# Attention and two MLPs on one core: the second MLP's weights are converted to float32 in DRAM beside blocks 1 to 4

## The chip, the core and the metric

The kernel runs on one core of a Trainium2 chip. A core has four engines that compute: TensorE (PE in the profile: matmuls, and PEld, its loading of weights), VectorE (DVE), ScalarE (ACT) and GpSimd (POOL); SyncE (SP) issues the transfers, which 16 DMA engines carry. Each engine works through its own queue in order. The metric is the time of one execution in microseconds (us).

## What is computed

Causal attention with a decay over 4 x 8 heads of 576 positions and 64 columns, then two MLPs on the 2304 x 512 result:

```python
scores = np.where(causal, -1e9, scale * q @ k.T + decay)
x  = softmax(scores) @ v                     # 2304 x 512, after moving heads
h  = x @ w_in                                # first MLP, 512 -> 2048
x  = (h * tanh(softplus(h))) @ w_out         # 2048 -> 512
h  = x @ w2_in                               # second MLP, 512 -> 1024
s  = h * softmax(h)
out = layernorm(s) * g_ln @ w2_out           # 1024 -> 512
```

The weights of both MLPs come as float64; all else is float32.

## The kernel before

Every float32 operand of a matmul is split into two float16 parts (high and low), and three products of parts make one product, so weights have to be converted and split before they are used. The result of attention is cut into 9 blocks of 256 rows (`TB`, `NBLK`). One loop runs over `hn`, two half steps for each of the 144 pieces of the first MLP (16 pieces of its 2048 columns a block): the first half step issues `up` (12 matmuls, line 754), the second one `mish_a` to `mish_c` on ScalarE, VectorE and POOL and `down` (6 matmuls of an earlier piece, line 798). Between them the loop issues the next slots of attention (scores, maximum, exponential, split, transpose by DMA, product with v), which run ahead of the block that needs them; attention ends in block 6.

A chunk of weights is 2 x 128 rows of 512 columns. The first MLP has 16 chunks, the second 8: four of `w2_in`, which go to the tile `w`, and four of `w2_out`, which go to `wo`. `Weight` handles them: `load` (line 123) brings the chunk as float64, 1 MB, into one of two staging buffers (`WB`); `conv` makes float32 of it with three VectorE operations on int32 views (lines 136, 138 and 140), in the place where the split will stand; for `w2_out` two VectorE operations (line 146) multiply the rows by `g_ln`; a square on ScalarE (line 149) leaves the sums from which `bound` takes the scale; `split` (lines 197 to 205) makes the two float16 parts, either with ScalarE and VectorE (`on_pool` 0) or with ScalarE for the scale and POOL for both parts (`on_pool` 1).

The first MLP's 16 chunks go through staging memory (`wst`) in the first 150 us, and that memory is then closed (line 913) and stays unused. When the last slot of attention has been issued, its memory is closed and `Stage2` takes it (here called the handover): its constructor makes a list of 26 steps, of which `prepare` takes one at every third half step (`S2E`): two loads, then conversions and loads in turn for both matrices, and for each matrix the bound and the four splits, all with POOL. When fewer than 9 steps are left (`S2R`) and at least 10 pieces have passed (`S2A`), `step` is called at every third piece: `first` (lines 991 to 1027) does the first product of a tile of 128 rows and all up to the layer norm, `second` (line 1037) the last product. What is left of the 18 tiles after the loop is done by `rest`.

The rows of the code are written in this order, and the program's scheduler then places each engine's instructions in the order in which it expects them to become ready; the queues run in that order.

## Time and profile before

| | |
|---|---|
| time, median of 3 runs (lowest, highest) | 861.41 us (856.87, 861.95) |
| the profiled execution's own time | 862.0 us |
| its span, first to last instruction | 860.2 us |
| busy: TensorE, VectorE | 748.2 us (87%), 606.7 us (71%) |
| busy: ScalarE, POOL | 549.1 us (64%), 442.2 us (51%) |
| granted TensorE clock, mean | 0.97 |

The shares are means over stages with different limits. In the first 180 us attention's first batch and the first MLP's weights fill VectorE; up to about 540 us the blocks of the first MLP and attention run beside each other; from there to about 600 us the first MLP runs beside the handover; after that the two MLPs, and at the end the second one alone, run on a full TensorE. A change is read from the stage in which it lies.

### The profile page before, as it was taken

How to read it: one execution, taken by the hardware profiler on the slowest of the kernel's cores; microseconds unless marked ns; L12 is line 12 of the kernel's file. 1: busy time of each engine (PE TensorE's matmuls, PEld its weight loads, DVE VectorE, ACT ScalarE, POOL GpSimd, SP SyncE). 2: the span in 40 equal slices, each digit the busy share in tenths (PEclk: the TensorE clock that was granted, in tenths of full speed). 3: DMA queues.
4: the chain of work that ended last, by engine and by line, in shares of the span. 5: the costliest groups of instructions: out<-in, count | busy, mean ns of one | idle time of the engine just before them, and what ended most of it. 6: DMA issues, size and time to landing. Idle time of an engine off the chain costs nothing.

```text
span 860.2 us, 16457 instructions
## 1 busy us (share of the span) xinstructions
PE 748.2 (87%) x6174; PEld 477.6 (56%) x6174; DVE 606.7 (71%) x1158; ACT 549.1 (64%) x1202; POOL 442.2 (51%) x341
## 2 busy tenths in 40 slices
PE   0555777789899988999999999986999999999997
PEld 0444545557567665676757677554555554444443
DVE  6699998597667878858887755599566444665451
ACT  5555657868778786888886767686955554333331
POOL 2268676755876576776678753228733122022110
PEclk9999997789999999999999999999999999999999
DMA  9999554487897889898896632841023423344543
GB/s 237 208 246 271 166 174 92 87 157 120 149 190 157 154 152 161 178 191 140 164 184 124 138 67 56 221 172 62 26 38 79 81 59 75 89 98 104 108 88 81
DMA packets 328571, 114.88 MB, mean 134 GB/s; under 512 B 317676, under 2 KB 317676, under 8 KB 328492
## 3 DMA queue, kind: packets, MB, share of 16 engines
q1 hardware_dynamic: 328492, 113.84, 63.2%
q8 instruction: 48, 0.79, 0.4%
q14 instruction: 31, 0.25, 0.1%
HBM read 46.59 MB, written 9.55 MB: 65 GB/s over the span
## 4 chain that ended last, share of the span: by engine, by line
PE 40%; DVE 23%; DMA 13%; ACT 9%; issue 8%; POOL 7%; SPq 1%; POOLq 0%; DVEq 0%; ACTq 0%
PE h L997 10%; PE o L1037 10%; PE x L798 9%; PE h L754 7%; DMA pT<-ph 4%; POOL ph L493 4%; DVE th L775 3%; DVE ta L771 2%; DMA w2i_r<-in_moe_w_in_dram 1%; DVE wout L140 1%; PE pv L524 1%; DVE ph L490 1%; DVE wout L138 1%; POOL gt L781 1%; DMA rawk<-in_k_dram 1%
## 5 line engine op out<-in xcount | busy, mean ns | idle before, releaser
L798 PE MATMUL x<-wout,gt 128*128 128x512 f16 x864 | 222.1, 392 | 21.8 <-ACT gt L780 10.1
L754 PE MATMUL h<-xT,win 128*128 128x256 f16 x1728 | 223.3, 279 | 2.3 <-POOL win L202 1.7
L493 POOL TENSOR_TENSOR ph<-p,ph 128x512 f16<-128x512 f32 (+4 forms) x120 | 159.6, 1334 | 80.3 <-ACT ph L492 32.8
L754 PEld LDWEIGHTS <-win 128*128 128x128 f16 x1728 | 170.3, 100 | 45.3 <-POOL win L202 1.8
L781 POOL TENSOR_TENSOR gt<-th,gt 128x512 f16<-128x512 f32 x72 | 91.9, 1277 | 100.5 <-ACT gt L780 100.5
L798 PEld LDWEIGHTS <-gt 128*128 128x128 f16 x864 | 81.6, 100 | 103.7 <-issue 14.9
L1025 POOL TENSOR_TENSOR z<-sl,z 128x1024 f16<-128x1024 f32 x18 | 38.7, 2150 | 138.1 <-DVE s2c L1004 111.3
L997 PE MATMUL h<-w,x2T 128*128 128x512 f16 x432 | 98.4, 380 | 2.9 <-POOL w L205 1.6
L1037 PE MATMUL o<-wo,zT 128*128 128x512 f16 x432 | 96.5, 379 | 0.5 <-DMA zT<-z 0.5
L410 PE MATMUL sp<-kt,qa 128*128 128x128 f16 (+3 forms) x480 | 71.8, 225 | 21.1 <-ACT p L454 11.9
L454 ACT ACTIVATE p<-sp,nm 64x64 f32<-64x64 f32 (+7 forms) x128 | 61.2, 484 | 41.0 <-DVE nm L452 23.3
L524 PE MATMUL pv<-vt,pT 128*128 128x64 f16 (+3 forms) x480 | 71.0, 203 | 15.4 <-DMA pT<-ph 10.7
L775 DVE SCALAR_TENSOR_TENSOR th<-ta,th 128x512 f32<-128x512 f32 x72 | 69.4, 965 | 21.1 <-ACT ta L774 20.9
L780 ACT CAST gt<-th 128x512 f16<-128x512 f32 x72 | 44.3, 615 | 48.6 <-DVE th L775 47.2
L411 PE MATMUL sp<-kt,qb 67*128 67x128 f16 (+3 forms) x480 | 72.9, 226 | 2.6 <-DVE qb L399 2.6
L997 PEld LDWEIGHTS <-x2T 128*128 128x128 f16 x432 | 42.3, 98 | 53.9 <-issue 4.0
L525 PE MATMUL pv<-vt,pT 128*128 128x64 f16 (+3 forms) x480 | 70.1, 198 | 1.0 <-DVE vt L198 1.0
L1037 PEld LDWEIGHTS <-zT 128*128 128x128 f16 x432 | 42.2, 98 | 51.5 <-DMA zT<-z 1.0
L526 PE MATMUL pv<-vt,pT 128*128 128x64 f16 (+3 forms) x480 | 70.3, 198 | 0.0
L772 ACT ACTIVATE ta<-ta 128x512 f32<-128x512 f32 x72 | 45.3, 631 | 36.0 <-DVE ta L771 35.8
L524 PEld LDWEIGHTS <-pT 128*128 128x128 f16 (+3 forms) x480 | 45.6, 102 | 36.7 <-DMA pT<-ph 20.5
L771 DVE TENSOR_SCALAR ta<-ta 128x512 f32<-128x512 f32 x72 | 53.7, 745 | 16.6 <-ACT ta L766 16.2
(235 smaller groups left out, 1455.8 us busy)
## 6 DMA issues: line engine op xcount, KB each, us to landing
wi_r<-in_moe_w_in_dram SPq DMA_DIRECT2D x8, 1024.0 KB
wo_r<-in_moe_w_out_dram SPq DMA_DIRECT2D x8, 1024.0 KB
rawk<-in_k_dram SPq DMA_DIRECT2D x25, 256.0 KB
rawv<-in_v_dram SPq DMA_DIRECT2D x25, 256.0 KB
x2d<-x2h SPq DMA_DIRECT2D x18, 256.0 KB
out_dram<-ro SPq DMA_DIRECT2D x18, 256.0 KB
w2i_r<-in_moe_w_in_dram SPq DMA_DIRECT2D x4, 1024.0 KB
w2o_r<-in_moe_w_out_dram SPq DMA_DIRECT2D x4, 1024.0 KB
```

Of the source, the lines that this page charges most:

```text
L410: nc.tensor.matmul(o, qa[:, h, r0:r1_], kc[:, h, a0:a1], start=True, stop=False)
L411: nc.tensor.matmul(o, qb_[:67, h, r0:r1_], kc[:67, H + h, a0:a1], start=False, stop=(c != i))
L493: nc.gpsimd.tensor_tensor(p4[:, :, 1], pv3, p4[:, :, 0], op=ALU.subtract)
L524: nc.tensor.matmul(o, pT[a0:a1, k, :m], vh, start=(c == 0), stop=False)
L526: nc.tensor.matmul(o, pT[a0:a1, k + 1, :m], vh, start=False, stop=(c == i))
L754: nc.tensor.matmul(ph, win[:, (fi // 4) * NC1 + c, col:col + P], x[:, lx * NC1 + c, :], start=(m == 0), stop=(m == 3 * NC1 - 1))
L771: nc.vector.tensor_scalar(ta, ta, E20, 1.0, op0=ALU.min, op1=ALU.add)
L775: nc.vector.scalar_tensor_tensor(th, ta, 2.5, th, op0=ALU.subtract, op1=ALU.mult)
L781: nc.gpsimd.tensor_tensor(gt[:, 1], th, gt[:, 0], op=ALU.subtract)
L798: nc.tensor.matmul(o, gt[:, lg, n % 2, t * P:(t + 1) * P], wout[:, fi, lw * 512:(lw + 1) * 512], start=(first and m == 0), stop=(last and ...
L997: nc.tensor.matmul(h[:, half * 512:(half + 1) * 512], x[:, lx * NC1 + c, :], self.w2[:, half * NC1 + c, lw * 512:(lw + 1) * 512], start=(n ...
L1037: nc.tensor.matmul(o, zT[:, lz * NF2 + c, :], self.wo[:, c, lw * 512:(lw + 1) * 512], start=(n == 0), stop=(n == 3 * NF2 - 1))
```

## The change

A new list of 25 steps, `pre`, is worked off in the loop once the first MLP's staging is closed: one step at every fourth half step from half step 36 on (`S2P0`, `S2PE`). Its first step opens a staging memory of one float64 buffer and one float32 buffer in the room of `wst`. Then each of the 8 chunks has three: its load; its conversion with the same three VectorE operations (now in `to_f32`) and, for `w2_out`, the two row scales; its square, with the float32 chunk's store to a DRAM tile `w2f`. `g_ln` is loaded at the start of the program. What is left of the list when attention ends would be done then.

`Stage2` reads the eight float32 chunks, 0.5 MB each, from `w2f` straight to the places where the splits take them, all eight issued at once, and has 10 steps left: two bounds and eight splits. Every second split uses ScalarE and VectorE and no longer POOL. `prepare` takes a step at every second half step, and the second MLP's tiles may start after 7 pieces and when fewer than 6 steps are left.

```diff
-S2A = 10
+S2A = 7
-S2R = 9
+S2R = 6
-S2E = 3
+S2E = 2
+S2P0 = 36
+S2PE = 4
...
+    def fetch(self, n):
+        self.nc.sync.dma_start(self.f32[:, 2 * n + 2:2 * n + 4].rearrange("p s e -> p (s e)"), self.src(n))
...
+    def pre_open(_):
+        pool = ea.enter_context(tc.tile_pool(name="w2c", bufs=1, side="right"))
+        nc.sync.dma_start(gl, g_ln.rearrange("(f p) -> p f", p=P))
+        wq["raw"] = pool.tile([P, 2, 512], w2_in.dtype, name="w2raw")
+        wq["f"] = pool.tile([P, 2, 512], F32, name="w2f32")
+    def pre_load(a):
+        nc.sync.dma_start(wq["raw"], part_of((w2_in, w2_out)[a[0]], a[1]))
+    def pre_conv(a):
+        w, n = a
+        raw, f = wq["raw"], wq["f"]
+        if raw.dtype != F32:
+            to_f32(nc, f, raw)
...
+        if w:
+            for s in range(2):
+                nc.vector.tensor_scalar(f[:, s], f[:, s], gl[:, 2 * n + s:2 * n + s + 1], None, op0=ALU.mult)
+    def pre_stat(a):
+        w, n = a
+        nc.scalar.activation(
+            wq["raw"].bitcast(F16)[:, :, :512], wq["f"], AF.Square, accum_out=w2st[:, w, n:n + 1])
+        nc.sync.dma_start(w2f[w, n], wq["f"].rearrange("p s e -> p (s e)"))
...
+        if wstp is None and pre and hn >= S2P0 and hn % S2PE == 0:
+            f, a = pre.pop(0)
+            f(a)
         if st2 is None and half and pos["k"] >= len(seq) + LAG:
+            while pre:
+                f, a = pre.pop(0)
+                f(a)
             ea.close()
-            st2 = Stage2(tc, es, w2_in, w2_out, g_ln, x2d, us2, out, ones)
+            st2 = Stage2(tc, es, w2f, w2st, x2d, us2, out, ones)
...
-        self.steps = [(a.load, n) for n in range(WB)]
-        for w, after in ((a, b), (b, None)):
+        for w in (a, b):
             for n in range(w.n):
-                self.steps.append((w.conv, n))
-                if n + WB < w.n:
-                    self.steps.append((w.load, n + WB))
-                elif after is not None:
-                    self.steps.append((after.load, n + WB - w.n))
+                w.fetch(n)
+        self.steps = []
+        for w in (a, b):
             self.steps.append((bound, w))
-            for n in range(w.n):
-                self.steps.append((w.split, n))
+            self.steps += [(lambda n, w=w: w.split(n, on_pool=n % 2), n) for n in range(w.n)]
```

Where the steps stand on the engines is decided by the scheduler. Three places, each as before and as now (line numbers differ, since the changed kernel's lines lie lower: 136, 138 and 140 are now 107, 109 and 111; 338, 96, 98 are 346, 98, 100; 300, 374, 396, 498 are 308, 382, 404, 506).

On VectorE, where the scales of attention's batch 1 are made (`sctkv`), before:

```order
L775 SCALAR_TENSOR_TENSOR th_1864<-ta_1863,th_1864 128x512
L338 TENSOR_SCALAR sctkv_1522<-sp_147 128x2
L96 TENSOR_SCALAR sctkv_1522<-sctkv_1522 128x2
L98 TENSOR_SCALAR sctkv_1522<-sctkv_1522 128x2
L340 RECIPROCAL sctkv_1522<-sctkv_1522 128x2
```

and now:

```order
L783 SCALAR_TENSOR_TENSOR th_1867<-ta_1866,th_1867 128x512
L107 TENSOR_SCALAR w2f_2070<-w2raw 128x1024
L346 TENSOR_SCALAR sctkv_1525<-sp_147 128x2
L109 SCALAR_TENSOR_TENSOR w2f_2070<-w2raw,w2f_2070 128x1024
L98 TENSOR_SCALAR sctkv_1525<-sctkv_1525 128x2
L111 SCALAR_TENSOR_TENSOR w2f_2070<-w2raw,w2f_2070 128x1024
L100 TENSOR_SCALAR sctkv_1525<-sctkv_1525 128x2
```

The second chunk's three operations (on `w2f`, from the staging `w2raw`) stand between the operations that make these scales.

On SP, behind the loads of batch 1's first rows (`rawv_0`), beside the transposes of attention's last rows of batch 0 (`pT`), before:

```order
L300 DMA rawv_0_1730<-in_v_dram 64x8x64
L498 DMA_TRANSPOSE pT_3_2_1193<-ph_3_2_1158 128x16x128
L498 DMA_TRANSPOSE pT_3_4_1288<-ph_3_4_1238 128x16x128
L498 DMA_TRANSPOSE pT_3_6_1382<-ph_3_6_1341 128x16x128
L498 DMA_TRANSPOSE pT_4_0_1504<-ph_4_0_1466 128x20x64
```

and now:

```order
L308 DMA rawv_0_1733<-in_v_dram 64x8x64
L891 DMA w2raw<-in_moe_w_in_dram 128x2x512
L506 DMA_TRANSPOSE pT_3_2_1196<-ph_3_2_1161 128x16x128
L506 DMA_TRANSPOSE pT_3_4_1291<-ph_3_4_1241 128x16x128
L908 DMA w2f<-w2f_2070 128x1024
L891 DMA w2raw<-in_moe_w_in_dram 128x2x512
L506 DMA_TRANSPOSE pT_3_6_1385<-ph_3_6_1344 128x16x128
L506 DMA_TRANSPOSE pT_4_0_1507<-ph_4_0_1469 128x20x64
L908 DMA w2f<-w2f_2070 128x1024
L891 DMA w2raw<-in_moe_w_in_dram 128x2x512
```

Three loads and two stores stand between the transposes; a store waits for its chunk's conversion, and the load behind it for that chunk's square.

On VectorE at the handover, behind the last operations of attention, before (`w2i_r` is a staging buffer, `w` the matrix):

```order
L136 TENSOR_SCALAR w_7366<-w2i_r_7412 128x1024
L138 SCALAR_TENSOR_TENSOR w_7366<-w2i_r_7412,w_7366 128x1024
L140 SCALAR_TENSOR_TENSOR w_7366<-w2i_r_7412,w_7366 128x1024
L771 TENSOR_SCALAR ta_7642<-ta_7642 128x512
L136 TENSOR_SCALAR w_7366<-w2i_r_7475 128x1024
L138 SCALAR_TENSOR_TENSOR w_7366<-w2i_r_7475,w_7366 128x1024
L140 SCALAR_TENSOR_TENSOR w_7366<-w2i_r_7475,w_7366 128x1024
L775 SCALAR_TENSOR_TENSOR th_7643<-ta_7642,th_7643 128x512
```

and now (`w2i_b` holds the first matrix's scale, `s2c` belongs to the second MLP's first tile):

```order
L184 TENSOR_SCALAR w2i_b<-sum_7471 128x1
L98 TENSOR_SCALAR w2i_b<-w2i_b 128x1
L100 TENSOR_SCALAR w2i_b<-w2i_b 128x1
L186 RECIPROCAL w2i_b<-w2i_b 128x1
L1011 TENSOR_SCALAR c_iw_7434<-w2i_b 128x1
L783 SCALAR_TENSOR_TENSOR th_7677<-ta_7676,th_7677 128x512
L187 TENSOR_SCALAR w2i_b<-w2i_b 128x1
L1049 TENSOR_TENSOR s2c_7802<-us_74,c_iw_7434 128x1
L1049 TENSOR_TENSOR s2c_7928<-us_74,c_iw_7434 128x1
L206 SCALAR_TENSOR_TENSOR w_7432<-w_7432,w2i_b 128x2x512
```

The conversions are gone; the first split (line 206) follows the scale of the first matrix.

## Rows read from the trace of the kernel before

**Rows 1.** Windows: length, busy us (instructions) of PE, PEld, DVE, ACT, POOL; clock, DMA share, GB/s.
```profile
537.50:559.00 21.50, 20.49 (x133) 12.68 (x132) 12.02 (x20) 14.48 (x27) 4.62 (x4) 1.00 0.81 219
559.00:580.50 21.50, 17.23 (x122) 11.57 (x121) 20.05 (x33) 17.34 (x32) 4.90 (x3) 1.00 0.49 174
580.50:602.00 21.50, 14.73 (x92) 9.02 (x90) 21.23 (x28) 14.04 (x23) 17.86 (x10) 0.92 0.18 62
602.00:623.50 21.50, 20.35 (x125) 12.09 (x124) 11.90 (x25) 19.79 (x33) 16.94 (x13) 1.00 0.10 26
623.50:645.00 21.50, 21.50 (x126) 12.22 (x125) 13.85 (x32) 12.14 (x22) 7.17 (x5) 1.00 0.25 38
```

**Rows 2.** Chain that ended last, in time, 527 to 603 us: start, us, what.
```profile
540.68 7.08 DMA w2i_r<-in_moe_w_in_dram
...
552.26 5.62 DMA w2i_r<-in_moe_w_in_dram
...
566.32 6.38 DMA w2o_r<-in_moe_w_out_dram
```

**Rows 3.** Windows, instructions on tile w, then on wo alone: PE, DVE, ACT, POOL busy us.
```profile
540.00:602.00 62.00, 4.13 (x14) 12.55 (x12) 8.84 (x12) 14.43 (x8) 0.97 0.49 153
...
540.00:602.00 62.00, 0.00 (x0) 20.84 (x20) 4.56 (x8) 0.00 (x0) 0.97 0.49 153
```

**Rows 4.** Source L149: duration ns min/median/max, first and last start, forms and counts.
```profile
L149 ACT ACTIVATE w2i_r<-w x4: 1041/1057/1057, 551.1 to 565.1; 128x1024 f16<-128x1024 f32 x4
...
L149 ACT ACTIVATE w2o_r<-wo x4: 1040/1048/1057, 572.3 to 599.2; 128x1024 f16<-128x1024 f32 x4
```

**Rows 5.** Source L198, the split's VectorE half on the first MLP's wout.
```profile
L198 DVE SCALAR_TENSOR_TENSOR wout<-wout,wo_b x4: 1269/1952/3064, 79.8 to 153.1; 128x1024 f16<-128x1024 f32 x4
```

**Rows 6.** DMA view of 537 to 600 us: GB/s in 40 slices.
```profile
GB/s 55 117 12 69 177 281 388 419 313 187 88 299 336 265 338 5 18 234 406 120 406 153 10 39 273 354 0 0 44 255 377 0 0 0 0 0 0 86 81 0
```

**Rows 7.** Chain that ended last, at the end of the program.
```profile
834.95 10.38 PE o L1037 x48
```

**Rows 8.** Timeline of SP's queue, 155 to 185 and 284 to 306 us: start, us, issue.
```profile
157.25 16.39 SPq L498 DMA_TRANSPOSE pT<-ph  x4
...
302.02 3.62 SPq L498 DMA_TRANSPOSE pT<-ph  x1
```

**Rows 9.** Windows, one stretch of 150 to 303 us, columns as in rows 1.
```profile
150.00:303.00 153.00, 135.92 (x1442) 97.06 (x1440) 111.80 (x217) 117.43 (x286) 101.90 (x84) 0.91 0.81 146
```

**Rows 10.** Source L138, the second conversion operation on w, handover.
```profile
L138 DVE SCALAR_TENSOR_TENSOR w<-w2i_r,w x4: 1225/1226/1234, 548.6 to 562.0; 128x1024 int32<-128x1024 int32 x4
```

**Rows 11.** VectorE groups, 60 to 140 us: count | busy us, mean ns | idle before.
```profile
L140 DVE SCALAR_TENSOR_TENSOR wout<-wo_r,wout 128x1024 int32<-128x1024 int32 x6 | 10.9, 1812 | 0.0
...
L138 DVE SCALAR_TENSOR_TENSOR wout<-wo_r,wout 128x1024 int32<-128x1024 int32 x6 | 10.8, 1802 | 0.0
...
L136 DVE TENSOR_SCALAR wout<-wo_r 128x1024 int32<-128x1024 int32 x6 | 6.9, 1153 | 0.1
```

**Rows 12.** VectorE groups, 540.7 to 602 us, columns as in rows 11.
```profile
L146 DVE TENSOR_SCALAR wo<-wo,gl 128x512 f32<-128x512 f32 x8 | 5.7, 737 | 0.0
```

**Rows 13.** Waits, 150 to 303 us: who for whom, us in total, times, longest.
```profile
POOL ph L493 <- DVE ph L490: 14.2, 10, 3.1
...
DVE ph L490 <- ACT p L454: 7.4, 5, 2.8
...
DVE nm L452 <- PE sp L413: 5.3, 6, 2.0
```

**Rows 14.** Chain that ended last, 150 to 303 us.
```profile
171.18 1.19 DVE sctkv L96
```

**Rows 15.** Chain that ended last, 90 to 150 us.
```profile
119.54 4.98 DMA wo_r<-in_moe_w_out_dram
```

**Rows 16.** Source L205, POOL's second split operation, columns as in rows 4.
```profile
L205 POOL TENSOR_TENSOR w<-w x4: 2127/2373/3098, 584.3 to 600.9; 128x1024 f16<-128x1024 f32 x4
L205 POOL TENSOR_TENSOR wo<-wo x4: 2125/2132/2135, 607.1 to 623.0; 128x1024 f16<-128x1024 f32 x4
```

More of the change, by code (lines that the diff above doesn't have):

```diff
@@ L98, in root2, with to_f32, __init__ @@
     nc.vector.tensor_scalar(dst, dst, 2.0 ** 64, None, op0=ALU.mult)
+def to_f32(nc, f, raw):
+    w = raw.bitcast(I32).rearrange("p s (e t) -> p s e t", t=2)
+    t = f.bitcast(I32)
+    nc.vector.tensor_scalar(
+        t, w[:, :, :, 1], 3, 0x3FFFFFF8, op0=ALU.logical_shift_left, op1=ALU.bitwise_and)
+    nc.vector.scalar_tensor_tensor(
+        t, w[:, :, :, 1], -0x40000000, t, op0=ALU.bitwise_and, op1=ALU.bitwise_or)
+    nc.vector.scalar_tensor_tensor(
+        t, w[:, :, :, 0], 29, t, op0=ALU.logical_shift_right, op1=ALU.bitwise_or)
 class Weight:
     last = None
-    def __init__(self, tc, pool, nm, dst, slots, src, across, group=None, row_scale=None, after=None, gram=None):
+    def __init__(self, tc, pool, nm, dst, slots, src, across, group=None, after=None, gram=None, stat=None):
         self.across = across
         self.tc, self.nc, self.pool, self.nm, self.dst, self.n = tc, tc.nc, pool, nm, dst, slots // 2
-        self.src, self.row_scale = src, row_scale
+        self.src = src
         self.group, self.after, self.gram = (group or slots) // 2, after, gram
@@ L114, in __init__ @@
         self.f32 = dst.rearrange("p s e -> p (s e)").bitcast(F32).rearrange("p (s e) -> p s e", e=512)
-        if gram is None:
+        self.stat = stat
+        if gram is None and stat is None:
             self.stat = pool.tile([P, self.n], F32, name=f"{nm}_stat")
@@ L133, in conv @@
         if self.f64:
-            w = raw.bitcast(I32).rearrange("p s (e t) -> p s e t", t=2)
-            t = f.bitcast(I32)
-            nc.vector.tensor_scalar(
-                t, w[:, :, :, 1], 3, 0x3FFFFFF8, op0=ALU.logical_shift_left, op1=ALU.bitwise_and)
-            nc.vector.scalar_tensor_tensor(
-                t, w[:, :, :, 1], -0x40000000, t, op0=ALU.bitwise_and, op1=ALU.bitwise_or)
-            nc.vector.scalar_tensor_tensor(
-                t, w[:, :, :, 0], 29, t, op0=ALU.logical_shift_right, op1=ALU.bitwise_or)
+            to_f32(nc, f, raw)
         else:
             nc.scalar.copy(f, raw)
-        if self.row_scale is not None:
-            for s in range(2):
-                nc.vector.tensor_scalar(
-                    f[:, s], f[:, s], self.row_scale[:, 2 * n + s:2 * n + s + 1], None, op0=ALU.mult)
         if self.gram is None:
@@ L868, in att_slots @@
         return min(max(x, lo), hi)
+    pre = []
+    w2f = dram.tile([2, NC1, P, 2 * 512], F32, name="w2f")
+    w2st = const.tile([P, 2, NC1], F32, name="w2st")
+    gl = const.tile([P, NF2], F32, name="gl")
+    def pre_open(_):
[9 more added lines that the diff above has]
+        if raw.dtype != F32:
+            to_f32(nc, f, raw)
+        else:
+            nc.scalar.copy(f, raw)
+        if w:
[6 more added lines that the diff above has]
+        nc.sync.dma_start(w2f[w, n], wq["f"].rearrange("p s e -> p (s e)"))
+    pre = [(pre_open, 0)]
+    for w in range(2):
+        for n in range(NC1):
+            pre += [(x, (w, n)) for x in (pre_load, pre_conv, pre_stat)]
     NF = NBLK * NF1
@@ L931, with __init__ @@
 class Stage2:
-    def __init__(self, tc, es, w2_in, w2_out, g_ln, x2d, us2, out, ones):
+    def __init__(self, tc, es, w2f, w2st, x2d, us2, out, ones):
         nc = tc.nc
@@ L946, in __init__ @@
         sp = self.es.enter_context(tc.tile_pool(name="w2s", bufs=1, side="right"))
-        gl = sp.tile([P, NF2], F32, name="gl")
-        nc.sync.dma_start(gl, g_ln.rearrange("(f p) -> p f", p=P))
         ps = self.es.enter_context(tc.tile_pool(name="ps2w", bufs=1, space=PSUM, side="right"))
@@ L954, in across @@
             return o
-        a = Weight(tc, sp, "w2i", self.w2, NC1 * DFF2 // 512, lambda n: part_of(w2_in, n), across)
-        b = Weight(tc, sp, "w2o", self.wo, NF2, lambda n: part_of(w2_out, n), across, row_scale=gl)
+        a = Weight(tc, sp, "w2i", self.w2, NC1 * DFF2 // 512, lambda n: w2f[0, n], across, stat=w2st[:, 0])
+        b = Weight(tc, sp, "w2o", self.wo, NF2, lambda n: w2f[1, n], across, stat=w2st[:, 1])
         def bound(w):
```

## The prediction

> **What bounds the kernel now.** I read the stretches of 21.5 us first, then the chain and VectorE's work in the worst of them, then the stretch that is to take the moved work.
>
> From 623.5 us on TensorE is busy 21.50 of every 21.50 us [rows 1]: nothing but its own work sets the end there, and the change leaves its matmuls alone. So the end moves only by what TensorE loses or gains before that. In the handover it loses: between 537.5 and 623.5 us it idles 1.01 + 4.27 + 6.77 + 1.15 = 13.2 us [rows 1]. In the two worst rows VectorE is busy 20.05 and 21.23 of 21.50 us, so it is what the others wait for. The chain shows with what: the second MLP's float64 loads take 7.08, 5.62 and 6.38 us on it [rows 2], two staging buffers at a time, and behind each load stand VectorE's conversions.
>
> **What is taken out of the handover.** The operations that write the two matrices keep VectorE busy for 12.55 and 20.84 us there [rows 3], 33.4 us in all: three operations a chunk, eight chunks, and eight row scales on the second. Eight squares on ScalarE of about 1.05 us go with them [rows 4]. Of the eight splits, which all ran on ScalarE (scale) and POOL (two operations), four go to ScalarE and VectorE. No row has that form for these tiles; the same operation on wout took 1.27 us at least and 3.06 at most [rows 5], so VectorE gets 5 to 12 us back. 21 to 28 of its 33.4 us are really gone. The bytes are halved: 4 MB of float32, issued at once, instead of 8 MB in pairs. One slice of the handover moved 419 GB/s [rows 6], by which 4 MB are 10 us; the first piece lands within the 7.08 us that its double took, so that the first split can run at about 548 us. In TensorE's order the first matmul of the second MLP stands after 1,310 of the 1,728 matmuls of line 754, where it stood after 1,440. I take the whole 13.2 us as the gain. Ends: 17 us if TensorE's busy time flatters it (a matmul that waits in its pipe counts as busy; the excess is my estimate), and 8 us if the first MLP's own ScalarE chain keeps some of it, as in the row from 537.5 us, where 1.0 us was lost with VectorE busy 12.02.
>
> That the second MLP starts earlier gives nothing beyond this: behind it TensorE is full in any order. After the last down projection four of its tiles are left where there were ten; at 5.19 us for 24 matmuls [rows 7] they are 41 us, which still cover the last tile's way through DRAM.
>
> **What is put into blocks 1 to 4.** The steps are written one to every four half steps, from half step 36 to 132, but the order decides. On SP the first load stands ahead of the transpose issued at 157.25 us, and the last store ahead of the one issued at 302.02 us [rows 8]. So all eight chunks land in 150 to 303 us, not spread over four blocks.
>
> *VectorE.* In that stretch it is busy 111.80 of 153.00 us [rows 9]: 41.2 us free. What a conversion lasts depends on POOL, and here is the main thing to see. On the first matrix in the handover, with POOL busy 4.62 and 4.90 of 21.50 us [rows 1], the large operations took 1.23 us each [rows 10]. Between 60 and 140 us, where the first MLP's weights go the same way beside attention's POOL work, the same operations average 1.80 and 1.81 us and the small one 1.15 [rows 11]. POOL is busy 101.90 of 153.00 us in the new place [rows 9], so I take these: 8 x (1.15 + 1.80 + 1.81) = 38.1 us, and eight row scales at their 0.74 [rows 12] = 5.9 us: 44.0 us. The lower bound, with POOL never in the way, is the handover's first matrix, 12.55 us for four chunks: 25.1 and 5.9, 31.0 us. VectorE's load becomes 156 us of 153, by the lower bound 143.
>
> *What of it passes.* VectorE's free time is made of waits, 7.4 us for ScalarE's exponentials and 5.3 for scores [rows 13], so a conversion that comes in order before such an operation is either in the gap or in the way. Others wait for VectorE in turn: POOL 14.2 us for its casts [rows 13], and behind POOL stand the transposes and TensorE. At one place it is surely in the way: the second chunk's three operations stand between those that make the scales of batch 1, which are on the chain at 171.18 us [rows 14]. For the rate I take the handover, the stretch where the trace shows what VectorE's conversions cost TensorE: 13.2 us lost for 33.4 us, 0.395. Then 44.0 x 0.395 = 17.4 us. Ends: nothing, if all of the lower bound falls into the 41.2 free; and 33 us, if three quarters of 44.0 pass.
>
> *ScalarE, SP, DMA.* Eight squares of 1.05 us go to ScalarE, which is busy 117.43 of 153.00 us [rows 4, 9]; its free 35.6 us cover them, at a price of 8.4 us if they don't. SP issues 8 loads and 8 stores more, in order: a store waits for its chunk's conversion, the next load for its square, and attention's transposes stand behind both. While the conversions are in time this costs the issue alone; where they are late it adds to their delay and is part of the rate above. Nothing for the bytes: in the early stretch a load of 1 MB lands in 4.98 us beside all other traffic [rows 15], and the chunks follow each other by 10 to 30 us.
>
> **Sum.** The profiled execution took 862.0 us (span 860.2): 862.0 - 13.2 + 17.4 = 866.2. It stands 0.6 us above the median of the runs, so **865.5 us**: the handover's gain is paid back a little more than whole, and a measurement will most likely not tell it from no change (about 1% is what it can tell).
>
> **A rule beside the trace.** First the rows: POOL's larger split operation, 128x1024, has a median of 2.37 us on w, beside the conversions, and of 2.13 on wo, after them; the longest are 3.10 and 2.14 [rows 16]. So conversions lengthen POOL's work as POOL lengthens theirs. The Trainium skill, page "SBUF — State Buffer", section "SBUF: two separate sides", says that VectorE operations with two SBUF inputs or in a two-port mode and GpSimd's operations take a shared port pair as an exclusive lock for a whole instruction, and the other one waits. The rows agree in direction, and the rule speaks against this change, which takes conversions from a place where POOL is idle to one where it is busy for two thirds. By the trace's medians a meeting costs POOL 0.24 us; by that rule, with the lock met half way on average, it would be 0.9 us, half of the 1.80 of the rows (an estimate from that page).
>
> **The rivals.**
> - *It fits into the gaps (faster).* Every engine but TensorE has a fifth of the stretch free or more, and 41.2 us are more than the lower bound of 31.0. Then at most a few us pass: with 2, 861.4 - 13.2 + 2 = 850. Against it: by the early rows VectorE's demand is 156 us of 153, and one chunk stands on the chain. It decides if the conversions last 1.3 us and not 1.8.
> - *POOL and VectorE hold each other up (slower).* Each of the 32 added VectorE operations costs POOL 0.24 to 0.97 us (median and longest over their undisturbed 2.13 [rows 16]); with the middle, 0.6, POOL's load rises by 19 us to 121, VectorE's by 44 to 156, both late at once, and three quarters of the 44.0 pass: 861.4 - 13.2 + 33 = 881. For it: the transposes' inputs come from POOL, and 14.2 us of its waits are for VectorE already. Against it: POOL has 51 us free. It decides from a loss of 22 us in the stretch on. The page named above would make this the likely one if every meeting cost the whole of the other's operation; the rows bear out a part of that.
> - *The handover keeps its loss.* If the first MLP's own ScalarE chain and not VectorE set it, only 4 us come back and 17 are paid: 874. Against it: in the row from 537.5 us TensorE loses 1.0 us.
>
> **How the numbers follow.** Forecast (rate about 0.4, from 856 to 871): 0.46. Fits: 0.23. Hold-up: 0.25. Handover keeps: 0.06. Nearly all of "fits" is faster by more than 1% (under 852.8 us): 0.22. Slower by more than 1% (over 870.0) are the hold-up, the last case and the forecast's upper edge: 0.33. The rest, 0.45, is within 1%. With 849 to 882 us no more than 2 in 10 is left out; the forecast's own range is 856 to 871.
>
> **What would show it.** In the profile after: (1) the handover's stretches, with TensorE idle under 3 us where 13.2 stood; (2) VectorE busy for 95% or more of the stretch from 150 us, the moved large operations at a mean of 1.6 us or more, and the transpose of 302.02 us issued 12 to 22 us later; (3) no wait of TensorE that is put down to the new loads or stores; (4) TensorE full from the second MLP's first tiles on. I am wrong if the conversions last 1.3 us there, or if that transpose comes less than 8 or more than 22 us later.

## The result, and the profile after

The changed kernel takes 867.1 us (median of 8 runs, 863.8 to 867.7) where the kernel before takes 860.1 us (8 runs, 856.9 to 862.0): ratio 1.0082, 95% interval 1.0058 to 1.0105. That is 7 us slower, inside the 1% that was called no change, and close to the forecast of 865.5 us. The profiled execution has a span of 865.8 us. The granted TensorE clock does not order the runs: 863.8 us came at a mean of 0.946 and 867.5 at 0.966. Below, us worked out from ratios are the ratio times 861.4 us.

The handover in the kernel after, as windows with the columns of [rows 1]:

```profile
537.50:559.00 21.50, 20.30 (x192) 14.64 (x191) 12.90 (x30) 17.08 (x34) 7.19 (x6) 1.00 0.26 56
559.00:580.50 21.50, 20.90 (x135) 12.88 (x133) 14.42 (x27) 19.18 (x30) 11.40 (x8) 1.00 0.75 233
580.50:602.00 21.50, 20.75 (x121) 11.52 (x120) 16.80 (x24) 13.45 (x25) 12.14 (x8) 1.00 0.24 49
602.00:623.50 21.50, 21.50 (x115) 11.03 (x114) 15.44 (x46) 12.88 (x25) 4.40 (x3) 1.00 0.29 76
```

TensorE's idle time there is 1.20 + 0.60 + 0.75 + 0 = 2.55 us where [rows 1] had 13.2, and VectorE, at 20.05 and 21.23 us before, is at 14.42 and 16.80.

The stretch that took the work in, as one window, against [rows 9]:

```profile
150.00:303.00 153.00, 127.58 (x1328) 92.04 (x1327) 125.20 (x209) 114.20 (x275) 100.59 (x77) 0.89 0.95 195
```

TensorE did 8.3 us less in the same time, with 114 fewer instructions. VectorE rose by 13.4 us only, with attention's own work pushed out of the stretch: the transpose that SP issued at 302.02 us [rows 8] now comes at 324.48, 22.5 us later.

The added work by line (duration in ns, minimum, median and maximum; first and last start), to be held against [rows 10 to 12] and [rows 4]:

```profile
L107 DVE TENSOR_SCALAR w2f<-w2raw x8: 679/899/1998, 161.6 to 313.9; 128x1024 int32<-128x1024 int32 x8
L109 DVE SCALAR_TENSOR_TENSOR w2f<-w2raw,w2f x8: 1206/1221/2060, 162.8 to 317.1; 128x1024 int32<-128x1024 int32 x8
L111 DVE SCALAR_TENSOR_TENSOR w2f<-w2raw,w2f x8: 1205/1212/2176, 164.9 to 318.8; 128x1024 int32<-128x1024 int32 x8
L906 ACT ACTIVATE w2raw<-w2f x8: 1050/1057/1059, 166.2 to 324.0; 128x1024 f16<-128x1024 f32 x8
L902 DVE TENSOR_SCALAR w2f<-w2f,gl x8: 473/482/1373, 242.1 to 323.5; 128x512 f32<-128x512 f32 x8
```

Lines 107, 109, 111 and 902 keep VectorE busy for 8.7, 10.9, 10.8 and 5.2 us: 35.6, and not the 44.0 that I forecast. New are, among others, these waits of SP, 150 to 330 us (who for whom, us in total, times, longest):

```profile
SPq L891 <- DVE wout L206: 4.8, 1, 4.8
SPq L908 <- DVE w2f L111: 4.4, 2, 2.8
SPq L908 <- DVE scu L354: 4.0, 1, 4.0
```

and of VectorE:

```profile
DVE w2f L107 <- DMA w2raw<-in_moe_w_in_dram: 4.1, 2, 2.7
DVE w2f L107 <- DMA w2raw<-in_moe_w_out_dram: 3.8, 1, 3.8
```

VectorE stands for 7.9 us at the first operation of a conversion until its chunk has landed, and SP stands at a first load (line 891) and at stores (line 908) with attention's transposes behind it. The timeline of SP's queue, 150 to 182 us, shows where [rows 8] had four transposes in a row (a row with x2 or x4 runs from its first start to its last end, waits included; alone, the four take 4.76, 1.87, 4.49 and 1.34 us here and 1.99, 1.93, 1.75 and 1.27 before):

```profile
155.65 0.38 SPq L891 DMA_DIRECT2D w2raw<-in_moe_w_in_dram  x1
156.63 6.73 SPq L506 DMA_TRANSPOSE pT<-ph  x2
166.15 0.35 SPq L908 DMA_DIRECT2D w2f<-w2f  x1
167.33 0.37 SPq L891 DMA_DIRECT2D w2raw<-in_moe_w_in_dram  x1
168.73 7.52 SPq L506 DMA_TRANSPOSE pT<-ph  x2
179.96 0.34 SPq L908 DMA_DIRECT2D w2f<-w2f  x1
181.14 0.37 SPq L891 DMA_DIRECT2D w2raw<-in_moe_w_in_dram  x1
```

### The profile page after: what moved, and what is told of

The parts are those of the page before. It is cut to its first block, busy times and chain, and to the rows that moved or that the text cites. A ratio compares the mean times of both kernels' runs of the same rounds, so it can differ in the third digit from the quotient of the medians.

```text
span 865.8 us, 16495 instructions
## 1 busy us (share of the span) xinstructions
PE 748.4 (86%) x6174; PEld 479.6 (55%) x6174; DVE 619.0 (71%) x1162; ACT 550.1 (64%) x1202; POOL 433.0 (50%) x333
## 4 chain that ended last, share of the span: by engine, by line
PE 29%; DVE 24%; DMA 16%; ACT 10%; issue 9%; POOL 9%; SPq 1%; POOLq 0%; DVEq 0%; ACTq 0%
PE h L1042 8%; PE o L1082 7%; PE x L806 6%; PE h L762 6%; DMA pT<-ph 5%; POOL ph L501 4%; DVE ta L779 2%; DMA qa<-qn 2%; POOL gt L789 1%; DMA w2raw<-in_moe_w_in_dram 1%; DVE th L783 1%; DMA rawk<-in_k_dram 1%; POOL xh L551 1%; POOL ph L496 1%; DVE ph L498 1%
## 5 line engine op out<-in xcount | busy, mean ns | idle before, releaser
L501 POOL TENSOR_TENSOR ph<-p,ph 128x512 f16<-128x512 f32 (+4 forms) x120 | 163.8, 1371 | 71.6 <-ACT ph L500 35.1
L806 PEld LDWEIGHTS <-gt 128*128 128x128 f16 x864 | 83.1, 100 | 88.0 <-issue 10.2
L418 PE MATMUL sp<-kt,qa 128*128 128x128 f16 (+3 forms) x480 | 72.5, 226 | 27.2 <-ACT p L462 10.7
L783 DVE SCALAR_TENSOR_TENSOR th<-ta,th 128x512 f32<-128x512 f32 x72 | 70.6, 980 | 33.0 <-ACT ta L782 32.2
```

What stands on the lines that cost most here:

```text
L418: nc.tensor.matmul(o, qa[:, h, r0:r1_], kc[:, h, a0:a1], start=True, stop=False)
L501: nc.gpsimd.tensor_tensor(p4[:, :, 1], pv3, p4[:, :, 0], op=ALU.subtract)
L783: nc.vector.scalar_tensor_tensor(th, ta, 2.5, th, op0=ALU.subtract, op1=ALU.mult)
L806: nc.tensor.matmul(o, gt[:, lg, n % 2, t * P:(t + 1) * P], wout[:, fi, lw * 512:(lw + 1) * 512], start=(first and m == 0), stop=(last and ...
```

## The experiments

Three explanations of the loss were set against each other: VectorE's operations themselves (A, V); VectorE waiting for loads through the one staging buffer (B); and the loads, stores and squares with SP's queue (C, T, S, Q). When the first four runs did not settle it, a fourth came up: that the added steps make the scheduler write everything else in another order (O). G and H say how much the handover gives back by itself. The table holds all runs; the third column is the ratio's distance from that of the pure handover, times 861.4 us; the last one is how much later than 302.02 us the transpose of [rows 8], the 35th of 72 `pT`, is issued in the profiled execution.

| kernel | ratio to before (interval) | over pure handover, us | transpose later by, us |
|---|---|---|---|
| the changed kernel | 1.0082 (1.0058, 1.0105) | 20.8 | 22.5 |
| e9, pure handover | 0.9841 (0.9812, 0.9871) | 0 | 0.2 |
| e10, small stores | 0.9876 (0.9846, 0.9906) | 3.0 | -3.9 |
| e1, handover and stores | 0.9959 (0.9938, 0.9979) | 10.2 | 3.2 |
| e2, no VectorE work | 0.9950 (0.9926, 0.9975) | 9.4 | 9.8 |
| e3, one load | 1.0132 (1.0107, 1.0157) | 25.1 | 28.6 |
| e4, two half buffers | 1.0067 (1.0038, 1.0096) | 19.5 | 25.8 |
| e6, spread | 1.0033 (1.0015, 1.0051) | 16.5 | 1.8 |
| e8, half buffers, spread | 1.0018 (0.9996, 1.0040) | 15.2 | -0.8 |
| f1, order kept | 1.0210 (1.0186, 1.0235) | 31.8 | 30.7 |
| f2, order kept, no VectorE work | 1.0108 (1.0070, 1.0145) | 23.0 | 22.5 |
| f4, order kept, one load | 1.0154 (1.0120, 1.0187) | 27.0 | 22.7 |
| g1, order kept, ScalarE's queue | 1.0287 (1.0257, 1.0317) | 38.4 | 36.0 |

An interval is some 2 to 3 us wide to each side, so differences under 4 us in the third column are not told apart. The last column comes from one execution; that of e6 took 861.2 us where its median is 864.9, so 3.7 us of its cost are not in its trace.

One reading goes through all of these traces, and it says where the loss arises. Here are the 72 transposes `pT` of attention's probabilities (duration in ns, minimum, median and maximum; first and last start) in the kernel before, in the changed kernel, in e9 and in f4:

```profile
L498 SPq DMA_TRANSPOSE pT<-ph x72: 1194/1723/4543, 36.1 to 527.7; - x72
L506 SPq DMA_TRANSPOSE pT<-ph x72: 1197/1940/5288, 35.9 to 546.8; - x72
L506 SPq DMA_TRANSPOSE pT<-ph x72: 1193/1759/4762, 35.7 to 527.4; - x72
L506 SPq DMA_TRANSPOSE pT<-ph x72: 1193/1812/4848, 35.8 to 551.6; - x72
```

Against e9 (span 846.4 us), the last of them starts 19.4 us later in the changed kernel, and its span is 19.4 longer; in f4 it is 24.2 and 23.8. In every run of the table the two agree within 1.6 us. So in these traces the whole loss is attention's delay up to its last transpose; the handover behind it passes the delay on and adds next to nothing.

### The handover alone (e1), and without VectorE's work (e2)

In e1 one filled tile is stored eight times:

```diff
-    for w in range(2):
-        for n in range(NC1):
-            pre += [(x, (w, n)) for x in (pre_load, pre_conv, pre_stat)]
+    def pre_fill(_):
+        nc.gpsimd.memset(wq["f"], 1.0)
+        nc.vector.memset(w2st, 1.0)
+        for w in range(2):
+            for n in range(NC1):
+                nc.sync.dma_start(w2f[w, n], wq["f"].rearrange("p s e -> p (s e)"))
+    pre += [(pre_fill, 0)]
```

In e2 only the conversion and the row scales go:

```diff
-            to_f32(nc, f, raw)
...
-                nc.vector.tensor_scalar(f[:, s], f[:, s], gl[:, 2 * n + s:2 * n + s + 1], None, op0=ALU.mult)
+        if a == (0, 0):
+            nc.gpsimd.memset(f, 1.0)
```

> Nothing is prepared in blocks 1 to 4: the eight float32 chunks in DRAM are stores of one tile filled with ones, so the second MLP's conversion, row scales and squares are left out; the handover is that of the changed kernel. It measures the handover's gain alone. All theories: if 13.2 us were to be had, 861 - 13 = 848 us; by the changed kernel's own trace (19 to 20 us late before the handover, 5 us late at the end) 846 to 847 us. Near 855 us, the handover gave back only half and the loss in the stretch was smaller than I read it.

> The changed kernel with its eight loads, squares and stores, but without VectorE's conversions and row scales (the second MLP's weights are ones). Theory A (VectorE's added operations and what stands behind them cost the 19 to 20 us): within 3 us of the run without any preparation, 847 to 850 us. Theory C (the transfers, the squares and SP's waits in order cost them): 858 us or more. Theory B (VectorE waiting for loads through one staging buffer) says what A says here.

Both came out near 858 us. For e1 this was far from 846 to 847, though its handover did what was expected: in its trace piece 96 of the first MLP's 144, the first one after attention's end, begins 10.8 us late and the program ends 2.8 us early (span 857.4 against 860.2). So something cost 10 us ahead of the handover with no conversion there at all. And e2, with loads, squares and stores but no work on VectorE, costs 9.4 us over the pure handover measured below: not the 3 us of theory A, and close to theory C.

### One load (e3), and two half buffers (e4)

e3 (its squares also write to a tile of their own), and below it e4 (its loads, conversions, squares and stores take half a chunk each, loads are written one piece ahead, and `S2PE` is 2); both are cut:

```diff
-        nc.sync.dma_start(wq["raw"], part_of((w2_in, w2_out)[a[0]], a[1]))
+        if a == (0, 0):
+            nc.sync.dma_start(wq["raw"], part_of(w2_in, 0))
...
```

```diff
-        wq["raw"] = pool.tile([P, 2, 512], w2_in.dtype, name="w2raw")
-        wq["f"] = pool.tile([P, 2, 512], F32, name="w2f32")
+        wq["raw"] = [pool.tile([P, 1, 512], w2_in.dtype, name=f"w2raw{i}") for i in range(2)]
+        wq["f"] = [pool.tile([P, 1, 512], F32, name=f"w2f32{i}") for i in range(2)]
...
```

> The changed kernel with all its VectorE operations, squares and stores, but only the first chunk is loaded and converted eight times, and the squares write to a tile of their own, so that no conversion waits for a load (7 of the second MLP's 8 chunks are left out). Theory A (the 35.6 us of VectorE operations themselves): as the changed kernel, 863 to 868 us. Theory B (the load, conversion, square, load chain through one buffer, with 8.0 us of VectorE standing at the first conversion): the loss of about 19 us falls to 10 or less, 852 to 858 us.

> The whole computation, with the preparation in 16 half chunks through two staging buffers and two float32 buffers of half the size, each load written one piece ahead, one step at every second half step. VectorE's time grows only by the fixed part of 28 more operations. Theory A: no better than the changed kernel, 866 to 871 us. Theory B: 855 to 861 us, with VectorE's waits for these loads under 3 us in place of 8.0.

Theory B asked for a gain of 8 us or more and there is none: e4 is where the changed kernel is, as theory A said, and e3, at 873.5 us, is 4 us slower than the changed kernel and above both theories' ranges. Two buffers did not even take the waits away: in e4 VectorE still stands for loads (waits, columns as above):

```profile
DVE w2f L107 <- DMA w2raw<-in_moe_w_in_dram: 3.8, 3, 2.4
DVE w2f L107 <- DMA w2raw<-in_moe_w_out_dram: 3.2, 3, 1.8
```

In e3, where seven of eight loads are gone, the conversions move earlier and the transpose is 28.6 us late. In the scheduler's own order, waiting through one buffer is not what costs by itself.

### The pure handover (e9), and small stores (e10)

In e9 the list of steps is empty and `qf` is q, seen as eight chunks:

```diff
-            st2 = Stage2(tc, es, w2f, w2st, x2d, us2, out, ones)
+            nc.vector.memset(w2st, 1.0)
+            st2 = Stage2(tc, es, qf, w2st, x2d, us2, out, ones)
```

e10 is e1 with `qf` and small stores:

```diff
-                nc.sync.dma_start(w2f[w, n], wq["f"].rearrange("p s e -> p (s e)"))
+                nc.sync.dma_start(w2f[w, n, :, :8], wq["f"][:, 0, :8])
```

> Nothing at all is put into blocks 1 to 4, not even stores: the handover of the changed kernel fetches its eight float32 chunks from q instead (the second MLP's conversion, row scales and squares are left out). Every engine's order up to the last slot of attention is that of the kernel before, word for word. Theory G (the handover itself gives back 13 to 14.5 us, and the run without conversions lost about 10 us of it elsewhere before 500 us): 846 to 849 us. Theory H (the handover gives only 4 us, as the time of that run alone says): 856 to 859 us.

> As the run with the handover alone, but the eight stores at 158 to 171 us carry 4 KB each instead of 0.5 MB, and the handover fetches from q (conversion, row scales and squares are left out as there). The bytes are gone; the steps still make the scheduler write attention's and the first MLP's instructions in another order from about 150 us on. Theory S (4 MB of stores in front of the transposes cost the 8 to 10 us that the run with the handover alone lost before 500 us): 846 to 849 us. Theory O (the other order costs them): 854 to 860 us.

e9 takes 847.4 us: 13.7 us less than before (11.1 to 16.2 by the interval), and theory G holds. Its windows, columns as in [rows 1]:

```profile
559.00:580.50 21.50, 20.75 (x121) 11.53 (x120) 17.39 (x24) 14.60 (x27) 13.78 (x9) 1.00 0.17 33
580.50:602.00 21.50, 21.50 (x120) 11.44 (x118) 14.95 (x45) 13.42 (x27) 3.87 (x3) 1.00 0.37 90
```

So the changed kernel loses 20.8 us by its preparation. e10 has the steps' disturbance of the order and nothing else to speak of, and costs 3.0 us, not told apart from none: this other order alone does not cost 8 to 10. Its 850.3 us lie between the two theories, nearer S. The 7 us between e10 and e1 are the 4 MB of stores or the further change of order that goes with them; these two were not separated.

### Spread over blocks 2 to 6 (e6, e8)

e8 has the same hold with the half buffers of e4 and `S2PE = 3`; this is e6:

```diff
-S2PE = 4
+S2PE = 6
...
-        nc.sync.dma_start(wq["raw"], part_of((w2_in, w2_out)[a[0]], a[1]))
+        i = nc.sync.dma_start(wq["raw"], part_of((w2_in, w2_out)[a[0]], a[1]))
+        if pend.get("pt"):
+            later(tc, i, pend["pt"])
```

> The whole computation with the changed kernel's preparation; each load is held on SP behind the transpose of attention written before it, and a step is taken at every sixth half step instead of every fourth, so the chunks land over blocks 2 to 6 (about 200 to 500 us) instead of 150 to 303 us. If VectorE's work costs by how full VectorE is in its stretch (it has 41 us free of 153 in 150 to 303 us, more after 500 us, and attention is further ahead by then): 855 to 861 us. If any place costs the same rate of 0.4 to 0.5 (35.6 us of operations): 862 to 868 us. If the scheduler's other order is what decides, it may come out anywhere from 852 to 872 us, without a tie to VectorE's busy time.

> As the run before it (loads held in written order, spread over blocks 2 to 6), but with the 16 half chunks through two staging and two float32 buffers, a step at every third half step. The waits for loads should be under 2 us in sum. By place and VectorE's free time: 852 to 859 us, a few us better than the spread with one buffer. If single-buffer waits never mattered: the same within 2 us.

Both are 4 to 6 us better than the changed kernel, and the best whole versions that were run; e8 is not told apart from the kernel before. e6's 864.9 us fall where the same rate at any place was forecast (and inside the wide range of the other order), and e8 is within 2 us of e6, as if single-buffer waits did not matter. What is instructive is the window 150 to 303 us, columns as in [rows 1], of e6:

```profile
150.00:303.00 153.00, 134.65 (x1448) 96.46 (x1447) 122.29 (x220) 118.90 (x290) 102.81 (x83) 0.94 0.86 167
```

and of e8:

```profile
150.00:303.00 153.00, 137.38 (x1459) 97.64 (x1458) 129.68 (x233) 121.19 (x301) 100.41 (x84) 0.93 0.88 169
```

VectorE carries 10.5 and 17.9 us more than in [rows 9] and the transpose of 302.02 us is not late: work of that amount does fit there when it comes thinly (about three of eight chunks in e6 and six of sixteen halves in e8). The rest fell due between 312 and 525 us, and the last transposes of attention come 12 us late. In e6 the last chunk is squared at 522.4 us only, but that late end costs the handover nothing: the span is 12.7 us over that of e9, and the last transpose 12.3 late. So nearly all of e6's delay came with the five chunks that fell due later, about 2 us each, where the changed kernel pays 2.6.

### Every other instruction held in the order before (f1, f2, f4)

`own` are all instructions up to the handover but those of the steps, and `e` is a table that gives them in the order of the kernel before; each is held behind the one before it on its engine, in issue alone. f2 and f4 add the edits of e2 and e3:

```diff
+    for k in e:
+        i = own[k]
+        if i.engine in last:
+            tc.add_manual_dep(
+                i, last[i.engine].name,
+                mybir.DependencyInfo(mybir.DependencyClass.NoSync, mybir.DependencyReason.DATA),
+                reason="issue order")
+        last[i.engine] = i
```

> The whole computation and the changed kernel's own steps, but everything else up to the end of attention is held in the order of the kernel before on all five engines; only the preparation's loads, conversions, squares and stores are slipped in between. Theory V (the added operations themselves, above all VectorE's 35.6 us, cost the 19 us over the pure handover's 847.4): 863 to 868 us. Theory O (most of it is that the added steps make the scheduler write all the rest in another order): 850 to 857 us.

> As the run before it, in the order of the kernel before, but without VectorE's conversions and row scales (the second MLP's weights are ones); loads, squares and stores stay. With the scheduler's own order this took 857.1 us, 9.7 over the pure handover. Theory T (the transfers, squares and SP's waits cost these 9.7): 855 to 859 us. Theory O (the other order did): 847 to 850 us.

> In the order of the kernel before, with all VectorE operations, squares and stores, but only one load, and squares that write to a tile of their own (7 of 8 chunks of the second MLP's weights are left out). Theory B (waits for loads through the one staging buffer): 4 to 8 us under the run that keeps order and loads. Theory A (VectorE's operations themselves): within 3 us of it.

Theory O expected the opposite of what came: in the old order the same work costs 31.8 us and not 20.8. The scheduler's new order had been saving 11 us. f1 and f2 came out above the ranges of all their theories. f4 is 4.8 us under f1 (the two intervals together make 3.6 us), which is what theory B forecast; but f4 leaves out the loads as well as the waits for them, so it does not show that the waits are what it saved. With the order held, the parts can be compared, and they do not add: loads, squares and stores without VectorE's work cost 23.0, VectorE's work, squares and stores behind one load 27.0, and all together 31.8. Whichever part is left out, most of the delay stays. In f1 the transpose of 302.02 us is 30.7 us late, the last one 32.3, and the span is 878.6 - 846.4 = 32.2 us over that of e9: nothing of it is caught up behind that point.

In f2 one reading is plain (SP's queue, 166 to 182 us):

```profile
162.90 3.33 SPq L506 DMA_TRANSPOSE pT<-ph  x1
166.33 0.53 SPq L891 DMA_DIRECT2D w2raw<-in_moe_w_in_dram  x1
166.91 4.55 SPq L903 DMA_DIRECT2D w2f<-w2f  x7
172.86 9.59 SPq L506 DMA_TRANSPOSE pT<-ph  x1
```

The transpose behind seven stores keeps SP for 9.59 us, where the same one in e9 takes 1.78:

```profile
166.07 1.78 SPq L506 DMA_TRANSPOSE pT<-ph  x1
```

The burst of seven belongs to this experiment (nothing holds the stores back when there is no conversion), so f2's and e2's share of the transfers is, if anything, too high. But the changed kernel has the same thing on a smaller scale, load by load (SP's queue, 225 to 236 and 289 to 298 us):

```profile
226.56 0.45 SPq L891 DMA_DIRECT2D w2raw<-in_moe_w_out_dram  x1
227.61 1.51 SPq L404 DMA_TRANSPOSE qa<-qn  x1
229.23 4.66 SPq L506 DMA_TRANSPOSE pT<-ph  x1
...
291.92 5.29 SPq L506 DMA_TRANSPOSE pT<-ph  x1
```

The chain that ended last has the load ahead of the last one (start, us, what):

```profile
290.25 6.70 DMA w2raw<-in_moe_w_out_dram
```

The load issued at 290.25 has landed at 296.95; the transpose issued behind it keeps SP until 291.92 + 5.29 = 297.21. From 150 to 330 us, 18 transposes of the changed kernel (11 of them `pT`) are issued while a chunk's load or store is on its way. They keep SP for 48.7 us, 2.7 each, where the other 26 take 1.6 each. Five of the 18 take over 4 us, and all five end within 0.3 us of the landing of a load.

How much of that is the copies' doing has to be held against the kernel before, where transposes are not always short either. There 15 of 54 in the same stretch take over 2 us with no chunk on its way; the longest, 4.54 us, stands behind three of attention's own smaller loads and ends 0.3 us after the last of them landed (SP's queue, 263 to 269 us):

```profile
263.20 0.87 SPq L300 DMA_DIRECT2D rawv<-in_v_dram  x1
264.25 4.54 SPq L498 DMA_TRANSPOSE pT<-ph  x1
```

The 24 transposes `pT` from the one at 157.25 us to the one at 302.02 [rows 8] keep SP for 48.6 us in the kernel before and in e9, and for 59.6 in the changed kernel: 11.0 more. But this sum and the delay do not go together. With one load it is 50.4 us (e3) and 50.3 (f4), hardly more than before, and the last of the 24 is 28.6 and 22.7 us late; in e2 it is 67.4, and the last one is 9.8 late. So the hold is real, and it is not what most of the loss needs.

### The same with ScalarE's queue (g1)

```diff
-        nc.sync.dma_start(wq["raw"], part_of((w2_in, w2_out)[a[0]], a[1]))
+        nc.scalar.dma_start(wq["raw"], part_of((w2_in, w2_out)[a[0]], a[1]))
...
-        nc.sync.dma_start(w2f[w, n], wq["f"].rearrange("p s e -> p (s e)"))
+        nc.scalar.dma_start(w2f[w, n], wq["f"].rearrange("p s e -> p (s e)"))
```

> The whole computation, as the run in the order of the kernel before (879.1 us, 31.7 over the pure handover), with one difference: the preparation's eight loads and eight stores are issued by ScalarE, each store right behind its chunk's square, instead of standing between attention's transposes on SP. ScalarE pays some 16 x 0.5 = 8 us for issuing. Theory Q (most of the loss is SP's queue: in that stretch SP issues transposes for 75 to 90% of the time, and every load and store that stands or waits there delays those behind it): the loss falls to the 8 us that VectorE's operations added beside the loads and stores, and a part of ScalarE's 8: 855 to 862 us. Theory V (VectorE's operations and the transfers themselves, on whatever queue): 872 to 880 us.

Theory Q falls: 887.1 us, 6.6 us more than f1, and above the range of theory V too. (Its premise was misread: transposes keep SP for 81.0 of the 163 us from 150 to 313 us of f1, half of the time and not 75 to 90%.) SP's queue holds no load or store of the preparation any more, and yet the first and the third transpose of [rows 8]'s four are held as before (SP's queue of g1, 156 to 161 and 168 to 175 us):

```profile
157.07 4.76 SPq L506 DMA_TRANSPOSE pT<-ph  x1
...
170.37 5.67 SPq L506 DMA_TRANSPOSE pT<-ph  x1
```

The first of the four in e9:

```profile
156.42 1.93 SPq L506 DMA_TRANSPOSE pT<-ph  x1
```

What these two wait for is the 1 MB copy on its way (issued by ScalarE at 156.06 and 168.31 us and landed 5.9 and 7.9 us later), not its place in SP's queue. The Trainium skill, page "DMA: Bandwidth & Descriptors", section "Issuing engines are not separate DMA queues", says that transfers of all issuing engines run on the same 16 DMA engines and that another issuer saves only the time of issuing; these rows agree. On VectorE the wait for loads grew; in g1 it is (150 to 313 us)

```profile
DVE w2f L107 <- DMA w2raw<-in_moe_w_in_dram: 10.6, 3, 3.8
```

where f1 has

```profile
DVE w2f L107 <- DMA w2raw<-in_moe_w_in_dram: 7.0, 3, 3.0
```

## Why the prediction came close, point by point

**The gain, 13.2 us: right.** e9 gives 13.7, all of it from the handover, and TensorE's idle time fell by 13.2 - 2.55 = 10.7 us in the changed kernel's windows. That this gain can be read as TensorE's idle time in [rows 1] and that a full TensorE behind it passes it on undiminished both held. That VectorE's conversions were its cause is not shown by itself: e9 takes out the conversions together with the float64 loads in pairs ahead of them [rows 2], and gives half of the splits to ScalarE and VectorE. The rival in which the handover keeps its loss is excluded.

**The loss, 17.4 us: 20.8 measured, from terms that were both mis-sized.**

- *What the conversions last.* I took [rows 11], 1.80 and 1.81 us, since POOL was busy both there and here. It is 1.36 on average, near [rows 10], and the sum 35.6 us instead of 44.0. What matters is not POOL's share but how its operations meet the conversion. Of the 16 large ones 12 took 1.20 to 1.23 us and four 1.4 to 2.2; those four all began with an operation of POOL under way, and only three of the 12 did. In [rows 11]'s stretch POOL ran splits of over 2 us one behind the other; here they are mostly attention's, whose costliest line (501) has a median of 1.34 us over the whole run.
- *What of it passes.* The rate 0.395, taken from the handover, was applied to VectorE alone. The changed kernel is 0.0132 of 861.4 us = 11.4 us slower than e2, in which only VectorE's work is missing: 11.4 of 35.6 us is 0.32. This holds as far as e2's transfers cost what they cost in the changed kernel, and the 11.4 hold VectorE's standing for loads too, since in e2 it waits for none. With the order held it is 31.8 - 23.0 = 8.8 us (f1 and f2).
- *ScalarE, SP, DMA at nothing: the step that failed.* "While the conversions are in time this costs the issue alone" was the sentence. e2 shows 9.4 us without any conversion. The trace shows two things that I had left out: a transpose that SP issues while a chunk's load is on its way can keep SP until the load has landed (11.0 us more over the 24 transposes above), and the loads, 5 to 8 us each, are late for VectorE (7.9 us of standing). I compared bytes with bandwidth, and the latency of one load with nothing. What e2's 9.4 us are made of is not shown: that standing is not among them, and e2 has a burst of stores that the changed kernel has not.

So, by e2, 11.4 + 9.4 us stand where 17.4 + 0 stood, and the sum hid it. That 865.5 us met 867.1 is luck to that extent: a term put at nothing was missing, and the one that was there came out too large.

**The rivals.** "Fits into gaps" was to be decided by conversions of 1.3 us; they last 1.36 and the loss is there. The condition was wrong: the length of the conversions was not what decided. For "POOL and VectorE hold each other up" the transpose is late by just over its 22 us, but not by its mechanism. POOL's load in the stretch is 100.59 us after 101.90, which alone says little, since work was pushed out; but all 283 of its operations up to attention's end take 357.1 us where they took 349.5 (348.0 in e9), 8 to 9 us more and not 19, and in f1, which loses the most but g1, they take 349.1.

**The signs.** (1) and (4) hold: 2.55 us idle, and no idle time from 602 to 840 us. (3) holds by its letter: no wait of TensorE is put down to a load or store of the preparation, while its wait for `pT` grew from 4.8 to 10.0 us (150 to 303 us, matmuls alone), which is the same thing seen one step later. (2) fails in all parts: VectorE is busy 125.20 of 153 us, 82% and not 95; the large operations take 1.36 us and not 1.6; and the transpose comes 22.5 us later, past the 22 that I had set as a limit. So by its own last sentence the prediction was wrong about the stretch, while its time was right.

**What stays open.** How the 20.8 us divide among the transposes that are held, VectorE's standing and VectorE's own operations is open; that they are attention's delay up to its last transpose is shown. On the chain that ended last, the changed kernel has from 150 to 547 us 18.6 us of the preparation's loads and 20.6 of its VectorE operations, so both lie on the path; what stood there before in their place is not known, so these are no prices. Leaving one out in the old order takes 5 to 9 of 31.8 us away; that the others keep the same chain late would explain it and was not shown. Why the scheduler's own order is 11 us better than the old one, and what of e1's 10.2 us is bytes and what order, was not tried. No version that does the work early and keeps the handover's 13.7 us was found.

## What to carry to other kernels

Price a stretch that is to take work in by running the other half alone: the kernel with the work left out (e9) gave the gain within 0.5 us of its forecast, and the distance to it is the price. Free time of each engine need not be room: 41.2 us were free on VectorE, 35.6 were put in, and 20.8 were lost. Leaving out one of several additions may show only a small part of their cost. And a copy of 1 MB can hold the DMA transposes issued behind it even where bandwidth is free, so look at them; but compare the same transposes before and after, for the longest hold need not be what makes the chain late. Halving the copies (e4) took the 11.0 us of hold to 6.3, and the kernel was not faster beyond the noise.

## What the runs showed of the hardware

**DMA transposes can wait for copies.** Issuing one takes SP 1.4 us in the median of the kernel before (150 to 330 us), with 1.2 as the least and 4.54 as the most. Behind a 1 MB load some take 4.1 to 5.7 us in the changed kernel and g1, and behind seven stores of 0.5 MB one took 9.59; the hold ended when the copy landed, within 0.3 us, in the cases read above, also when another engine had issued the copy. Not every transpose behind a copy is held: the one at 227.61 us took 1.51 us, and only the next, at 229.23, was; behind the load issued at 181.14 three in a row took 1.2 to 1.3. Which are held is open. The Trainium skill, page "Perfetto Trace Analysis", section "DMA Instruction — HWDGE (DVE, Sync)", says that the shown span of such an instruction begins when its semaphores are satisfied and includes waiting for the descriptor generator; that agrees with a hold that shows as issue and not as a wait.

**A small VectorE operation can take as long as a large one.** Timeline of VectorE in the changed kernel, 172 to 180 us:

```profile
175.47 2.06 DVE L109 SCALAR_TENSOR_TENSOR w2f<-w2raw,w2f 128x1024 int32<-128x1024 int32 x1
177.45 1.36 DVE L98 TENSOR_SCALAR sctkv<-sctkv 128x2 int32<-128x2 int32 x1
178.72 1.21 DVE L111 SCALAR_TENSOR_TENSOR w2f<-w2raw,w2f 128x1024 int32<-128x1024 int32 x1
179.85 0.15 DVE L100 TENSOR_SCALAR sctkv<-sctkv 128x2 f32<-128x2 f32 x1
```

and of POOL:

```profile
174.84 1.60 POOL L789 TENSOR_TENSOR gt<-th,gt 128x512 f16<-128x512 f32 x1
176.41 2.37 POOL L501 TENSOR_TENSOR ph<-p,ph 64x640 f16<-64x640 f32 x1
```

Two columns take 1.36 us, until POOL's operation of 176.41 ends at 178.78, and the next operation of that size takes 0.15. Line 109 started 0.63 us after POOL's operation of 174.84 and ended 2.06 later, 0.85 over its usual 1.21; that POOL operation ended 0.97 us after the start. So here whichever is first goes through and the other waits, which is what the page "SBUF — State Buffer" of the Trainium skill says in its section "SBUF: two separate sides"; here the trace agrees, and the 1.19 us of [rows 14] are the same thing on the kernel before. It does not show in every meeting: at 164.91 and 239.25 us line 111 began 0.68 and 0.18 us behind an operation of POOL and took its usual 1.21. In this change the large operations of a conversion became 0.15 us longer on average, and the small one 0.4 (1.09 against 0.68).
